# Starting the down projection one burst later in batch 2 of a fused attention and ReGLU kernel

## The chip, the cores and the metric

The kernel runs on one core of one Trainium2 chip. The metric is device time in microseconds of one launch. All inputs and the output are float32 in the chip's DRAM; the matrix products inside run on float16 tiles with float32 sums.

## The reference: what is computed

```python
# q, k, v: (8 batches, 12 heads, 448 positions, 64)
scores = scale * np.matmul(q, k.transpose(0, 1, 3, 2)) - np.log(S)      # scale = 1/8, S = 448
attn = 1.0 / (1.0 + np.exp(-scores))                                    # a sigmoid, no softmax
attn_out = np.matmul(attn, v)
x = attn_out.transpose(0, 2, 1, 3).reshape(B * S, H * D)                # (3584, 768)

# w_gate, w_val: (768, 1536), w_out: (1536, 768)
gate = np.maximum(x @ w_gate, 0.0)
val = x @ w_val
out = gate * val @ w_out                                                # (3584, 768)
```

For each batch there are scores, a sigmoid and a product with V (the attention), and then a feed-forward part: gate and value projections, their product h, and a down projection with `w_out`.

## The kernel before: the parts that matter

The order of instructions on TensorE is written by hand, batch after batch. Attention of batch b is interleaved with feed-forward work that earlier batches have left in two queues. A `gv` piece ("f" in the code) makes one 128-wide slice of h for one batch; there are 12 of them for each batch. A `down` tile ("y") makes 128 finished rows of the output from all 12 slices of h of a pair of batches; there are 7 of them for each pair, and the first pair is batches 0 and 1.

```python
def gv(b, q0, qn, f, act_relu):                      # "f"
    ps = []
    for nm, wt in (("g_ps", wg), ("v_ps", wv)):
        ps.append(bank(nm))
        for dc in range(NDC):                        # 6 matmuls each
            nc.tensor.matmul(ps[-1][:, 0:qn], wt[:, dc, f*P:(f+1)*P],
                             xT_tiles[(b, dc)][:, q0:q0+qn], start=..., stop=...)
    ...                                              # Relu on ScalarE, then VectorE writes hT
    nc.vector.tensor_tensor(out=hT_tiles[(g, f)][:, o:o+qn], in0=gate_sb[:, 0:qn],
                            in1=ps[1][:, 0:qn], op=AOP.mult)

def down(g, t):                                      # "y"
    ...
    for nm, m0, m1 in (("ya", 0, 512), ("yb", 512, DM)):
        ps = bank(nm)
        for f in range(NFC):                         # 12 matmuls each
            nc.tensor.matmul(ps[:, 0:m1-m0], hT_tiles[(g, f)][:, t*P:(t+1)*P],
                             wo[:, f, m0:m1], start=..., stop=...)
        nc.vector.tensor_scalar(out=ysb[:, m0:m1], in0=ps[:, 0:m1-m0], scalar1=OUT_SCALE, ...)
    store(g, t, ysb, 0, DM, (nc.sync, nc.sync))
```

`bank` hands out the eight PSUM banks in turn, two rings of four each. The weights `wo` of the down projection come in two transfers, columns 0 to 511 for `ya` and columns 512 to 767 for `yb`. They are issued by GpSimd late in batch 1, behind a small copy (`hold`) that waits for a transposed tile of batch 2, and behind V of batch 2:

```python
def load_o():
    for m0, m1 in ((0, 512), (512, DM)):
        nc.gpsimd.dma_start(wo[:, :, m0:m1], moe_w_out[:, m0:m1].rearrange("(c p) m -> p c m", p=P))

def hold(b, g):
    nc.gpsimd.tensor_copy(gate[0:1, :], qkT_tiles[(b, g)][0:1, 0, 0:2])

def late_loads():                                    # a hook in the last burst of batch 1
    dma_transposes(2, 1)
    hold(2, 1)
    load_v(2)
    load_o()
```

A batch is cut into six bursts, m = 0 to 5. A burst is three or four score units (`qk_unit`: 4 matmuls, then two sigmoids on ScalarE, for one chunk of 64 keys), with a product with V (`pv_group`) placed after the second unit in some bursts, and then the feed-forward pieces that `mix[m]` names:

```python
for b in range(1, B):
    cuts = (0, 3, 6, 9, 13, 17, 21) if b == 1 else (0, 4, 7, 11, 14, 18, 21)
    pv_at = {3: 0, 5: 1} if b == 1 else {0: -1, 2: 0, 4: 1}
    ...
    elif b == 2:
        mix = ["ff", "ff", "ffy", "ff", "ffy", "ffy"]
    elif b % 2:
        mix = ["ffy", "ffy", "ff", "ffy", "ff", "ffy"]
    else:
        mix = ["ffy", "ff", "ffy", "ff", "ffy", "ff"]
    for m in range(len(mix)):
        for i, (g, c) in enumerate(order[cuts[m] : cuts[m + 1]]):
            if i == 2 and m in pv_at:
                if m == 0: pv_finish(b - 1)
                else:      pv_group(b, pv_at[m])
            qk_unit(b, g, c)
        if m >= 4 and 1 < b < B - 1:
            dma_transposes(b + 1, m - 4)             # VectorE copies k, q to rel; SyncE issues the transpose
        if m == 0 and b > 1:
            dma_transposes(b, 2)
        ...
        elif m == 0 and b + 1 < B:
            if b == 2: hold(2, 2)
            load(b + 1, 0, 3, "kq")                  # k and q of the next batch, by GpSimd
            load_v(b + 1)
        ffn_mix(mix[m], hooks.get(m, ()))
```

After batch 7 whatever is left in the two queues is worked off.

Of the kernel before, what the change touches and what calls it, by code (L numbers as in the profile page):

```python
# [17 lines left out]
def kernel(  # L18
# [74 lines left out]
    def load(b, g0, g1, which, c0=0, c1=NCH):  # L93
        for nm, t16, src in zip("kq", tiles_of(b), (k, q)):
            if nm in which:
                xs, cs = slice(2 * g0, 2 * g1), slice(c0 * D, c1 * D)
                nc.gpsimd.dma_start(t16[:, xs, cs], rows_of(src, b)[:, xs, cs])  # L97

    def load_v(b):
        v16 = tiles_of(b)[2]  # L100
        nc.gpsimd.dma_start(v16[:, 0::2, :], rows_of(v, b)[:, 0::2, :])  # L101
        for r in range(2):
            nc.gpsimd.dma_start(  # L103
                v16[64 - 64 * r : P - 64 * r, 1::2, :], rows_of(v, b)[64 * r : 64 * r + 64, 1::2, :]
            )
# [95 lines left out]
    def dma_transposes(b, g):  # L201
        k16, q16, _ = in_tiles[b]
        rel = relp.tile([P, TW, P], FP16, tag="rel", name="rel")
        for ti, t16 in enumerate((k16, q16)):
            nc.vector.tensor_copy(
                rel[:, ti * NCH : (ti + 1) * NCH, :].rearrange("p c (h d) -> p h c d", h=2),
                t16[:, 2 * g : 2 * g + 2, :].rearrange("p h (c d) -> p h c d", c=NCH),
            )
        nc.sync.dma_start_transpose(
            qkT_of(b, g)[:], rel[:].rearrange("p c x -> p (c x)")  # L210
        )
# [68 lines left out]
    def qk_unit(b, g, c):  # L280
        ps = [bank("qk_ps") for _ in range(2)]
        qk(qkT_tiles[(b, g)], c, 0, NCH, lambda hh: ps[hh][:, 0:S])
        PT = PTp.tile([P, 2, 512], FP16, tag="PT", name="PT")
        for hh in range(2):
            sigmoid(PT[:, hh, 0:S], ps[hh][:, 0:S])
        PT_tiles[(b, g, c)] = PT

    def pv_group(b, g):
        pv(b, g, 0, S, [PT_tiles.pop((b, g, c))[:, :, 0:S] for c in range(NCH)])
# [81 lines left out]
    def ffn_mix(kinds, hooks=()):  # L371
        hooks = list(hooks)
        for left in range(len(kinds), -1, -1):
            while hooks and hooks[0][0] >= left:
                hooks.pop(0)[1]()
            if left:
                (gv_queue if kinds[len(kinds) - left] == "f" else y_queue).popleft()()
# [58 lines left out]
    def pv_finish(b):  # L436
        pv_group(b, NG - 1)
        push_gv(b, 0, S, range(NFC))
        if b % 2:
            push_down(b // 2, range(7))  # L440
# [5 lines left out]
    def hold(b, g):  # L446
        nc.gpsimd.tensor_copy(gate[0:1, :], qkT_tiles[(b, g)][0:1, 0, 0:2])

    def both(b, g):
        pe_transposes(b, g, 0)  # L450
        pe_transposes(b, g, 1)
# [8 lines left out]
# [3 lines that stand above are left out]
        hooks = {}  # L463
        if b == 1:
            mix = ["f" * n for n in (3, 3, 3, 3, 3, 2)]
            hooks = {
                1: [(1, lambda: both(1, 1))],
                3: [(1, lambda: both(1, 2))],
                4: [(3, lambda: dma_transposes(2, 0))],
                5: [(2, late_loads)],  # L470
            }
        elif b == 2:
            mix = ["ff", "ff", "ffy", "ff", "ffy", "ffy"]
        elif b % 2:
            mix = ["ffy", "ffy", "ff", "ffy", "ff", "ffy"]
        else:
# [4 lines that stand above are left out]
                    if m == 0:  # L481
                        pv_finish(b - 1)
                    else:
                        pv_group(b, pv_at[m])
                qk_unit(b, g, c)
            if m >= 4 and 1 < b < B - 1:
                dma_transposes(b + 1, m - 4)
            if m == 0 and b > 1:
                dma_transposes(b, 2)
            if b == 1:  # L490
                if m == 0:
                    load(2, 0, 1, "kq")
                    load(2, 1, 2, "kq")
                    load(2, 2, 3, "kq")
            elif m == 0 and b + 1 < B:
                if b == 2:
                    hold(2, 2)
                load(b + 1, 0, 3, "kq")
                load_v(b + 1)
            ffn_mix(mix[m], hooks.get(m, ()))  # L500
# [34 lines left out]
```

## Time and profile before

| what | value |
|---|---|
| time, median of 3 runs | 431.05 us (430.83 to 431.26) |
| span of the profiled execution | 429.5 us |
| TensorE matmuls (PE) | 418.5 us busy, 97% of the span |
| VectorE (DVE) | 141.8 us, 33% |
| ScalarE (ACT) | 201.1 us, 47% |
| GpSimd (POOL) | 49.8 us, 12% |
| granted TensorE clock | 1.000 |

In the profile's lines PE is the matmul stream of TensorE and PEld its weight loads, which overlap the matmuls. A name such as `ya<-wo,hT` means that the instructions write the tile `ya` and read `wo` and `hT`; L335 is the source line of the matmul in `down`, L297 that in `gv`, L222 that in the score units, L240 that in the product with V. "x12" counts instructions. A bracket at the end of a timeline line is the idle time of the engine ahead of that line, and what ended it. In a timeline the second column is how long the merged group lasted up to the modelled end of its last instruction, so that groups can overlap slightly.

### The profile page before, as it was taken

To read this page: it belongs to the slowest core of one execution; us is meant where nothing else is said; L and a number is where in the kernel's file an instruction comes from. 1 tells how busy PE (TensorE), PEld (TensorE's weight loads), DVE (VectorE), ACT (ScalarE), POOL (GpSimd) and SP (SyncE) were. 2 spreads that over 40 slices of the span, in tenths; PEclk is the share of its full clock that TensorE was granted. 3 is DMA by queue.
4 is the path that set the end of the run, shared out by engine and by line. 5 is a ranking of instruction groups with operands and counts; after the bars stand their busy time and mean duration, and the time that the engine had idled before them with its cause. 6 is when DMAs were issued, how large, how long until landed. Compare 5 with 4: busy or idle time off the path is not lost.

```text
span 429.5 us, 8576 instructions
## 1 busy us (share of the span) xinstructions
PE 418.5 (97%) x3668; PEld 231.9 (54%) x3668; DVE 141.8 (33%) x277; ACT 201.1 (47%) x424; POOL 49.8 (12%) x73
## 2 busy tenths in 40 slices
PE   8899999889999999999999999999999999999996
PEld 3677774345555455545545455545545554555563
DVE  2453443224233243233242243332442322322231
ACT  5766787434444454446443743473473446122000
POOL 9543204400030001200030000100000000000000
PEclk9999999999999999999999999999999999999999
DMA  9999958999799033951389114721243101100134
GB/s 147 198 202 203 203 81 131 203 220 195 110 155 182 0 81 82 169 104 38 85 122 182 46 43 82 127 56 38 44 88 75 37 2 38 37 2 0 46 102 110
DMA packets 68789, 43.63 MB, mean 102 GB/s; under 512 B 35600, under 2 KB 65168, under 8 KB 68752
## 3 DMA queue, kind: packets, MB, share of 16 engines
q0 software_dynamic: 30736, 23.37, 36.5%
q1 hardware_dynamic: 37664, 19.47, 22.7%
q8 instruction: 28, 0.46, 0.4%
q10 hardware_dynamic: 352, 0.26, 0.2%
q14 instruction: 9, 0.07, 0.1%
HBM read 47.19 MB, written 11.01 MB: 136 GB/s over the span
## 4 chain that ended last, share of the span: by engine, by line
PE 78%; DMA 13%; issue 5%; POOL 3%; DVE 0%; ACT 0%; POOLq 0%
PE g_ps L297 21%; PE v_ps L297 21%; PE ya L335 16%; PE yb L335 9%; PE qk_ps L222 6%; PE pv_ps L240 5%; DMA wo<-in_moe_w_out_dram 4%; DMA v<-in_v_dram 4%; DMA q<-in_q_dram 3%; DMA wg<-in_moe_w_gate_dram 2%; POOL k L97 1%; POOL q L97 1%; POOL v L103 1%; POOL v L101 0%; DVE xT L168 0%
## 5 line engine op out<-in xcount | busy, mean ns | idle before, releaser
L177 ACT ACTIVATE PT<-qk_ps 128x448 f16<-128x448 f32 (+3 forms) x318 | 151.6, 584 | 123.2 <-PE qk_ps L222 122.3
L297 PE MATMUL g_ps<-xT,wg 128*128 128x448 f16 (+2 forms) x648 | 127.5, 333 | 0.2 <-DVE xT L168 0.2
L297 PE MATMUL v_ps<-xT,wv 128*128 128x448 f16 (+2 forms) x648 | 126.8, 332 | 0.3 <-DMA wv<-in_moe_w_val_dram 0.3
L315 DVE TENSOR_TENSOR hT<-gate_sb,v_ps 128x448 f16<-128x448 f32 (+2 forms) x108 | 61.0, 569 | 164.5 <-PE v_ps L297 98.0
L335 PEld LDWEIGHTS <-hT 128*128 128x128 f16 x672 | 65.6, 98 | 50.6 <-DMA wo<-in_moe_w_out_dram 4.0
L297 PEld LDWEIGHTS <-wg 128*128 128x128 f16 x648 | 58.4, 98 | 56.5 <-issue 15.8
L297 PEld LDWEIGHTS <-wv 128*128 128x128 f16 x648 | 62.3, 98 | 47.9 <-DMA wv<-in_moe_w_val_dram 0.6
L306 ACT ACTIVATE gate_sb<-g_ps 128x448 f32<-128x448 f32 (+2 forms) x102 | 54.4, 544 | 70.8 <-PE g_ps L297 70.6
L335 PE MATMUL ya<-wo,hT 128*128 128x512 f16 x336 | 77.1, 379 | 1.9 <-DMA wo<-in_moe_w_out_dram 1.9
L222 PE MATMUL qk_ps<-qkT 64*64 64x448 f16 (+2 forms) x756 | 48.0, 336 | 1.9 <-ACT PT L177 1.1
L335 PE MATMUL yb<-wo,hT 128*128 128x256 f16 x336 | 41.3, 273 | 1.2 <-DMA wo<-in_moe_w_out_dram 1.2
L168 DVE TENSOR_SCALAR xT<-pv_ps 128x448 f16<-128x448 f32 (+2 forms) x54 | 28.4, 568 | 30.8 <-PE pv_ps L240 30.8
L343 DVE TENSOR_SCALAR ysb<-ya 128x512 f32<-128x512 f32 x28 | 19.4, 692 | 56.9 <-PE ya L335 55.0
L240 PE MATMUL pv_ps<-PT,v 64*64 64x448 f16 (+2 forms) x756 | 36.7, 329 | 0.0
L222 PEld LDWEIGHTS <-qkT 64*64 64x64 f16 x756 | 17.8, 105 | 21.6 <-issue 14.3
L240 PEld LDWEIGHTS <-v 64*64 64x64 f16 x756 | 21.6, 107 | 10.8 <-issue 0.5
L101 POOL DMA_DIRECT2D v<-in_v_dram x8 | 6.0, 747 | 174.2 <-PE qk_ps L222 173.9
L343 DVE TENSOR_SCALAR ysb<-yb 128x256 f32<-128x256 f32 x27 | 11.5, 425 | 18.1 <-PE yb L335 18.1
L349 ACT ACTIVATE ysb<-yb 128x256 f32<-128x256 f32 x1 | 0.4, 384 | 27.9 <-PE yb L335 27.9
L97 POOL DMA_DIRECT2D q<-in_q_dram x15 | 11.4, 760 | 8.8 <-PE trt L191 2.9
L97 POOL DMA_DIRECT2D k<-in_k_dram x14 | 10.9, 778 | 7.6 <-DMA wv<-in_moe_w_val_dram 3.5
L103 POOL DMA_DIRECT2D v<-in_v_dram x16 | 10.1, 635 | 2.6 <-DMA wg<-in_moe_w_gate_dram 2.3
(25 smaller groups left out, 59.4 us busy)
## 6 DMA issues: line engine op xcount, KB each, us to landing
out_dram<-ysb SPq DMA_DIRECT2D x54, 192.0 KB, 2.7
k<-in_k_dram POOLq DMA_DIRECT2D x5, 672.0 KB, 13.7
q<-in_q_dram POOLq DMA_DIRECT2D x5, 672.0 KB, 17.0
v<-in_v_dram POOLq DMA_DIRECT2D x8, 336.0 KB, 5.3
v<-in_v_dram POOLq DMA_DIRECT2D x16, 168.0 KB, 6.6
k<-in_k_dram POOLq DMA_DIRECT2D x8, 224.0 KB, 10.4
wo<-in_moe_w_out_dram POOLq DMA_DIRECT2D x1, 1536.0 KB, 15.4
q<-in_q_dram POOLq DMA_DIRECT2D x6, 224.0 KB, 11.2
```

The lines of the kernel that those rows point to most:

```text
L97: nc.gpsimd.dma_start(t16[:, xs, cs], rows_of(src, b)[:, xs, cs])
L101: nc.gpsimd.dma_start(v16[:, 0::2, :], rows_of(v, b)[:, 0::2, :])
L103: nc.gpsimd.dma_start(v16[64 - 64 * r : P - 64 * r, 1::2, :], rows_of(v, b)[64 * r : 64 * r + 64, 1::2, :])
L168: nc.vector.tensor_scalar(out=xT_of(b, pr)[:, q0 : q0 + qn], in0=src, scalar1=XSCALE, scalar2=None, op0=AOP.mult,)
L177: nc.scalar.activation(PT_ap, ps_ap, AF.Sigmoid, bias=sig_bias, scale=qk_scale)
L222: nc.tensor.matmul(out_of(hh)[o : o + 64, :], qkT[rows, c, cols], qkT[rows, NCH + c0 : NCH + c1, cols], start=True, stop=True, tile_positi ...
L240: nc.tensor.matmul(ps[hh][64 * r : 64 * r + 64, 0:qn], v16[rows, 2 * g + hh, c * D : (c + 1) * D], pieces[c][rows, hh, :], start=(c == 0), ...
L297: nc.tensor.matmul(ps[-1][:, 0:qn], wt[:, dc, f * P : (f + 1) * P], xT_tiles[(b, dc)][:, q0 : q0 + qn], start=(dc == 0), stop=(dc == NDC - 1),
L306: nc.scalar.activation(gate_sb[:, 0:qn], ps[0][:, 0:qn], AF.Relu)
L315: nc.vector.tensor_tensor(out=hT_tiles[(g, f)][:, o : o + qn], in0=gate_sb[:, 0:qn], in1=ps[1][:, 0:qn], op=AOP.mult,)
L335: nc.tensor.matmul(ps[:, 0 : m1 - m0], hT_tiles[(g, f)][:, t * P : (t + 1) * P], wo[:, f, m0:m1], start=(f == 0), stop=(f == NFC - 1),)
L343: nc.vector.tensor_scalar(out=ysb[:, m0:m1], in0=ps[:, 0 : m1 - m0], scalar1=OUT_SCALE, scalar2=None, op0=AOP.mult)
```

## The change

In batch 2 the mix of feed-forward work is reordered: the first down tile stands in burst 3 instead of burst 2, and the other two stay where they were, in bursts 4 and 5. It gives the two transfers of `wo` one burst more before the first matmul that reads them. Nothing is added or taken away.

```diff
         elif b == 2:
-            mix = ["ff", "ff", "ffy", "ff", "ffy", "ffy"]
+            mix = ["ff", "ff", "ff", "ffy", "ffy", "ffy"]
         elif b % 2:
```

The engines' instruction lists differ in only that: on TensorE the 24 matmuls of the first down tile, with their weight loads, come 36 matmuls later (12 of three score units and 24 of two `gv` pieces), and on VectorE the two copies of the tile out of PSUM come behind the two `hT` products of burst 3 instead of ahead of them. The lists of ScalarE, GpSimd and SyncE are the same in both kernels.

## The prediction

> **What bounds the kernel now.** I read the busy shares of the page first, then the list of what TensorE waited for, then TensorE's timeline around the longest of those waits, then the transfers and VectorE near it. The shares:
>
> ```profile
> PE 418.5 (97%) x3668; PEld 231.9 (54%) x3668; DVE 141.8 (33%) x277; ACT 201.1 (47%) x424; POOL 49.8 (12%) x73
> ```
>
> The matmul stream sets the time. The kernel can only gain by shorter matmuls or fewer gaps between them; this change leaves every matmul as it is, so only gaps count. The list of TensorE's waits over the whole kernel, in full but for its head:
>
> ```profile
> PE ya L335 <- DMA wo<-in_moe_w_out_dram: 1.9, 1, 1.9
> PE yb L335 <- DMA wo<-in_moe_w_out_dram: 1.2, 1, 1.2
> PE warm_ps L160 <- DVE zeros L116: 1.2, 1, 1.2
> PE qk_ps L222 <- ACT PT L177: 1.1, 4, 0.4
> PE qk_ps L222 <- DVE qkT L196: 0.8, 2, 0.5
> PE v_ps L297 <- DMA wv<-in_moe_w_val_dram: 0.3, 1, 0.3
> PE g_ps L297 <- DVE xT L168: 0.2, 1, 0.2
> PE trt L191 <- DVE k L383: 0.2, 1, 0.2
> ```
>
> The two largest are the first down tile waiting for the two halves of its weights, 3.1 us together. Asked by stretches, the same list puts all the others but one in the first 30 us (the `xT` one, 0.2 us, comes after 250 us). So after the start the kernel has one real hole. TensorE's timeline across it, then across burst 4, where a down tile does not wait (start, duration, engine, line, operation):
>
> ```profile
> 82.04 1.30 PE L297 MATMUL v_ps<-xT,wv 128*128 128x448 f16 x6
> 85.25 2.76 PE L335 MATMUL ya<-wo,hT 128*128 128x512 f16 x12 [1.91 <-DMA wo<-in_moe_w_out_dram]
> 89.22 1.48 PE L335 MATMUL yb<-wo,hT 128*128 128x256 f16 x12 [1.20 <-DMA wo<-in_moe_w_out_dram]
> 90.63 0.76 PE L222 MATMUL qk_ps<-qkT 64*64 64x448 f16 x12
> ...
> 95.97 0.57 PE L222 MATMUL qk_ps<-qkT 64*64 64x448 f16 x8
> ...
> 101.59 1.30 PE L297 MATMUL v_ps<-xT,wv 128*128 128x448 f16 x6
> 102.73 2.75 PE L335 MATMUL ya<-wo,hT 128*128 128x512 f16 x12
> 105.32 1.47 PE L335 MATMUL yb<-wo,hT 128*128 128x256 f16 x12
> 106.72 0.76 PE L222 MATMUL qk_ps<-qkT 64*64 64x448 f16 x12
> ```
>
> The reader should compare starts, not ends. In burst 4 `ya` begins 102.73 - 101.59 = 1.14 us after the last `v_ps` group, `yb` 2.59 us after `ya`, and the next scores 1.40 us after `yb`. In the waiting tile the same distances are 85.25 - 82.04 = 3.21, 89.22 - 85.25 = 3.97 and 1.41. The hole is thus (3.21 - 1.14) + (3.97 - 2.59) = 2.07 + 1.38 = 3.45 us, a little more than the 3.1 us of the wait list, which counts from modelled ends.
>
> **What the Trainium skill says.** "Perfetto Trace Analysis", section "Tensor Engine Instruction (MATMUL, LD_WEIGHTS)", says that a matmul's reported end is computed and not observed; the trace agrees, since 82.04 + 1.30 = 83.34 while an unhindered successor starts at 83.18. I therefore take the 3.45. "TensorE: Matmul & The Clock Gate", section "Back-to-back issue gap", gives N/2.4 + 2.5 ns for an isolated warm matmul, 215.8 ns at N = 512; here 2.59 us / 12 = 216 ns, so the tile itself has nothing left to lose. "PSUM — Partial Sum Buffer", section "Engine vs sequencer instructions", says that matmuls start in program order: so nothing behind the waiting tile could slip ahead, and the order has to be changed by hand. The trace agrees: no score matmul starts between 82.04 and 90.63. "DMA: Bandwidth & Descriptors", section "Anatomy of one DMA — SWDGE (gpsimd) path", says that waits happen on the issuing sequencer and that DMA engines only consume their queues; a load already issued is then not moved by a shift on TensorE. That fixes the landing times used below.
>
> **The change, part by part.** It removes and adds no instruction.
>
> First, the slot left empty. Burst 2's last `v_ps` starts at 82.04, and burst 3's scores follow it as scores follow a burst without a down tile: in burst 1 to 2 of the same batch, 76.42 - 75.19 = 1.23 us. They start at 82.04 + 1.23 = 83.27 instead of 90.63.
>
> Second, what now precedes the tile. Burst 3 takes 95.97 - 90.63 = 5.34 us from its scores to the next scores; 0.09 of it is the step from `gv` to scores (1.23 - 1.14), so `ya` can begin after 5.25 us, at 88.52, and `yb` at 88.52 + 2.59 = 91.11.
>
> Third, whether the weights are there. GpSimd issues the halves at 69.84 and 70.90; they take 15.4 and 18.3 us from issue to landing and land at 85.2 and 89.2 (the matmuls start within 0.1 us of that). Nothing ahead of 83.2 us differs between the kernels, so these times hold. Slack is 88.52 - 85.2 = 3.3 us for `ya` and 91.11 - 89.2 = 1.9 us for `yb`. Both waits vanish whole.
>
> Fourth, the sum. The tile takes 2.59 + 1.40 = 3.99 us, so burst 4's scores begin at 88.52 + 3.99 = 92.51 instead of 95.97: 3.46 us earlier, the hole again but for rounding. From there both orders are identical, and each later gap would have to be new to give something back. All of the gain lies on the path that sets the end, because TensorE runs without a hole from there to the last down tile.
>
> **The rivals.** The first: a load with a fixed arrival becomes the next wait. The candidates are k and q of batch 3, issued while `wo` is still moving; q is the later. Its issue on GpSimd, its time to landing (last column of the transfers issued in that stretch), and the copies on VectorE that read both:
>
> ```profile
> 79.63 0.83 POOL L97 DMA_DIRECT2D q<-in_q_dram x1
> ```
> ```profile
> q<-in_q_dram POOLq DMA_DIRECT2D x1, 672.0 KB, 17.0
> ```
> ```profile
> 98.97 0.38 DVE L205 COPY rel<-k 128x896 f16<-128x896 f16 x1
> 99.27 0.39 DVE L205 COPY rel<-q 128x896 f16<-128x896 f16 x1
> 100.73 0.62 DVE L315 TENSOR_TENSOR hT<-gate_sb,v_ps 128x448 f16<-128x448 f32 x1 [1.07 <-PE v_ps L297]
> ```
>
> q lands at 79.63 + 17.0 = 96.6. Today its copy comes 2.6 us later; after the shift it would want to start at 99.27 - 3.45 = 95.8 and so waits 0.8 us. This new wait I do expect. But it is VectorE's: it ends near 97.0, and the next product is due at 100.73 - 3.45 = 97.3. Even if q came 1 us later, the `hT` product only frees a PSUM bank eight groups on, over 4 us later. The transposed tile made from these copies, 9.5 us from issue to landing (so at about 107), is first read in batch 3's scores, at 115.96 - 3.45 = 112.5. I put the cost at 0; were it wrong and fully exposed, it would be 0.8 us, giving 428.4.
>
> The second: the hole gave ScalarE time to rest (8.3 us idle), and score units now come close behind `gv` pieces, so TensorE could wait for sigmoids to free PSUM banks; the list shows 1.1 us of that in four waits. Against it: those are in the first 30 us, and the step from burst 1 of batch 2 to burst 2, again three score units after `ff` with no tile between, shows no idle bracket, though ScalarE has eight sigmoids there (3.60 us in its timeline, 0.45 us each). If it came all the same, a wait like the largest there (0.4 us) would leave 428.0.
>
> The third: the `wo` landing is delayed, so that the tile waits again. For: the loads share the 16 DMA engines, and two of 192 KB each for the output are issued at 91.19, later in the new kernel. Against: stores come after `yb`, when `wo` is in. To lose all 3.45 us the second half would have to come 5.4 us late; I give that one chance in a hundred.
>
> The fourth: the tile only moves to where it hurts the tail. The queues are drained in the same order after batch 2, and the last tiles are the same, so the end is not touched.
>
> **Range and chances.** 431.05 - 3.45 = 427.6 us, which is 0.8% less. The three runs of before span 0.43 us, so noise of the median is some 0.2 us on each side; new small waits can only take from the gain, up to 0.8 us. I take 427.2 to 428.4. A gain over 2% would need 8.6 us, more than all of TensorE's waits together; a loss of 2% has no source. Chances: 0.01, 0.98, 0.01.
>
> **What would show it right or wrong.** In the changed kernel's waits of TensorE the two `wo` lines should be gone and nothing over 0.4 us should be new. The timeline should show burst 3's scores at about 83.3, `ya` at 88.5, `yb` at 91.1, burst 4's scores at 92.5, and a span near 426.0 instead of 429.5. On VectorE a wait of about 0.8 us for q ahead of its copy to `rel`, near 96.6, with no wait of TensorE behind it. The prediction is wrong if a line for `wo` stays, if scores start to wait for `PT`, or if burst 4 is 3.5 us early and the last tile is not.

## The result and the profile after

The changed kernel takes 427.89 us (median of 4 runs, 427.89 to 428.94) against 430.97 us (4 runs, 430.83 to 431.26) for the kernel before: 3.1 us less, a ratio of 0.9934 with a 95% interval of 0.9917 to 0.9951. The span of the profiled execution goes from 429.5 to 426.0 us.

The list of what TensorE waited for, in full, answers the list of the kernel before:

```profile
PE warm_ps L160 <- DVE zeros L116: 1.2, 1, 1.2
PE qk_ps L222 <- ACT PT L177: 1.1, 4, 0.4
PE qk_ps L222 <- DVE qkT L196: 0.8, 2, 0.5
PE g_ps L297 <- DVE xT L168: 0.2, 1, 0.2
PE v_ps L297 <- DMA wv<-in_moe_w_val_dram: 0.2, 1, 0.2
```

The two lines for `wo` are gone and no line is new. TensorE's timeline over the same place shows what filled the hole:

```profile
82.07 1.30 PE L297 MATMUL v_ps<-xT,wv 128*128 128x448 f16 x6
83.30 0.76 PE L222 MATMUL qk_ps<-qkT 64*64 64x448 f16 x12
...
87.41 1.30 PE L297 MATMUL v_ps<-xT,wv 128*128 128x448 f16 x6
88.54 2.75 PE L335 MATMUL ya<-wo,hT 128*128 128x512 f16 x12
91.13 1.47 PE L335 MATMUL yb<-wo,hT 128*128 128x256 f16 x12
92.53 0.57 PE L222 MATMUL qk_ps<-qkT 64*64 64x448 f16 x8
```

Burst 3's scores follow burst 2's `f` pieces at once, `ya` comes 1.13 us after the last `v_ps`, `yb` 2.59 us after `ya`, and no line has a bracket of idle time. Burst 4's scores start at 92.53 instead of 95.97, 3.44 us earlier. Nothing was given back over the remaining 325 us: the last down tile's `ya` starts 3.43 us earlier too. Before, then after:

```profile
421.44 2.75 PE L335 MATMUL ya<-wo,hT 128*128 128x512 f16 x12
```
```profile
418.01 2.75 PE L335 MATMUL ya<-wo,hT 128*128 128x512 f16 x12
```

On VectorE, the copies that read k and q of batch 3:

```profile
95.54 0.38 DVE L205 COPY rel<-k 128x896 f16<-128x896 f16 x1
96.08 0.39 DVE L205 COPY rel<-q 128x896 f16<-128x896 f16 x1 [0.16 <-DMA q<-in_q_dram]
97.29 0.62 DVE L315 TENSOR_TENSOR hT<-gate_sb,v_ps 128x448 f16<-128x448 f32 x1 [0.81 <-PE v_ps L297]
```

The wait for q is new, as foreseen, and is over 1.2 us before the next product.

### The profile page after: what moved, and what is told of

The parts are those of the page before. It is cut to its first block, busy times and chain, and to the rows that moved or that the text cites. A ratio compares the mean times of both kernels' runs of the same rounds, so it can differ in the third digit from the quotient of the medians.

```text
span 426.0 us, 8576 instructions
## 1 busy us (share of the span) xinstructions
PE 418.5 (98%) x3668; PEld 232.1 (54%) x3668; DVE 141.8 (33%) x277; ACT 200.9 (47%) x424; POOL 49.7 (12%) x73
## 4 chain that ended last, share of the span: by engine, by line
PE 93%; DMA 3%; POOL 2%; ACT 0%; DVE 0%; issue 0%; POOLq 0%; ACTq 0%
PE g_ps L297 26%; PE v_ps L297 25%; PE ya L335 17%; PE yb L335 9%; PE qk_ps L222 8%; PE pv_ps L240 7%; DMA wv<-in_moe_w_val_dram 3%; POOL q L97 1%; PE trt L191 1%; POOL k L97 1%; POOL wg L133 0%; POOL v L103 0%; DVE xT L168 0%; ACT PT L177 0%; POOL wv L134 0%
## 5 line engine op out<-in xcount | busy, mean ns | idle before, releaser
L343 DVE TENSOR_SCALAR ysb<-yb 128x256 f32<-128x256 f32 x27 | 11.5, 425 | 16.7 <-PE yb L335 16.7
## 6 DMA issues: line engine op xcount, KB each, us to landing
q<-in_q_dram POOLq DMA_DIRECT2D x5, 672.0 KB, 16.5
```

What stands on the lines that cost most here:

```text
L343: nc.vector.tensor_scalar(out=ysb[:, m0:m1], in0=ps[:, 0 : m1 - m0], scalar1=OUT_SCALE, scalar2=None, op0=AOP.mult)
```

## The experiments

The theory: the gain is the vanished wait for the two halves of `wo`, nothing else; what counts is when each half lands against when its matmuls come up. The main rival: the order of bursts is worth something by itself (a tile in burst 3 fits better, or more delay helps). A second rival: a late transfer elsewhere eats into the gain. All comparisons are with the kernel before, or with the changed kernel, run on the same chip in the same series where there was one; between series the kernel before stood at 430.97, 431.55, 431.28 and 431.28 us.

### The tile at two places inside burst 3

```diff
-            mix = ["ff", "ff", "ff", "ffy", "ffy", "ffy"]
+            mix = ["ff", "ff", "ff", "yff", "ffy", "ffy"]     # e3
+            mix = ["ff", "ff", "ff", "fyf", "ffy", "ffy"]     # e4
```

> The down tile placed in burst 3 right behind the three score units, ahead of both f pieces (yff). ya could begin at 83.3 + 0.7 = 84.0 us and waits 1.3 us for the first half (landing 85.3); yb could begin 2.59 later at 87.8 and waits until 89.2. Against the changed kernel the tile's end is 89.2 + 1.4 - (84.0 + 3.99) = 2.6 us late. Theory (only landing times count): 427.9 + 2.6 = 430.5 us, span 428.6. Rival (one burst of delay is what counts, the tile being in burst 3 either way): 427.9.

> The down tile in burst 3 between the two f pieces (fyf). ya begins at 84.0 + 2.27 = 86.3 us, after the first half is in: no wait. yb could begin at 88.85 and waits until 89.2 to 89.3. Theory: one wait for wo, of yb, 0.3 to 0.5 us, and 427.9 + 0.4 = 428.3 us, span 426.4. Rival: 427.9 with no wait, or 431 if the tile needs the whole burst ahead of it.

With the tile right behind the scores: 430.55 us (20 runs; ratio 0.9977, 0.9970 to 0.9985), span 428.4. Its timeline:

```profile
83.37 0.76 PE L222 MATMUL qk_ps<-qkT 64*64 64x448 f16 x12
85.09 2.76 PE L335 MATMUL ya<-wo,hT 128*128 128x512 f16 x12 [0.96 <-DMA wo<-in_moe_w_out_dram]
89.03 1.48 PE L335 MATMUL yb<-wo,hT 128*128 128x256 f16 x12 [1.17 <-DMA wo<-in_moe_w_out_dram]
90.35 1.30 PE L297 MATMUL g_ps<-xT,wg 128*128 128x448 f16 x6
```

By starts, `ya` waits 85.09 - 83.37 - 0.70 = 1.02 us (0.70 is the step from such scores to what follows them) and `yb` 89.03 - 85.09 - 2.59 = 1.35, together 2.37. The span is 428.4 - 426.0 = 2.4 us over the changed kernel's, and the median is 431.55 - 430.55 = 1.0 us under the kernel before. The tile stands in burst 3 here too and most of the gain is lost, so the burst is not what counts.

With the tile between the two `f` pieces: 428.66 us (4 runs, 428.06 to 429.25; ratio 0.9936, 0.9919 to 0.9954). In its profile `ya` starts at 87.44 and `yb` at 90.23, 2.79 us apart instead of 2.59, so 0.2 us of wait for the second half; the list of waits doesn't show it, since the modelled end of `ya` covers it. Expected were 0.3 to 0.5. The tile stands later than foreseen because this whole execution runs 1.2 us late; the issue of `wo`, at 71.04 instead of 69.89, is late with it. The median cannot carry a wait of 0.2 us, because its runs fall into two groups, 428.06 and 428.14 against 429.18 and 429.25. The profile is of the 429.25, and its list has waits at the start that the first profile of the changed kernel has not or has shorter: 0.6 us for `wv`, 0.4 for V, 0.2 for k.

### `wo` early, in both orders

```diff
     def late_loads():
         dma_transposes(2, 1)
         hold(2, 1)
         load_v(2)
-        load_o()
...
             if b == 1:
                 if m == 0:
                     ...
                     load(2, 2, 3, "kq")
+                    load_o()
```

> The old order of down tiles, but both wo transfers issued in burst 0 of batch 1, right behind k and q of batch 2, instead of behind V of batch 2. Estimated landing: k and q of batch 2 are in at 56.5 us, wo's 2304 KB at some 204 KB per us take 11.3 more, so about 68 us, before the first ya at 83.2. Theory (the gain is the vanished wait for wo and nothing else): no wait for wo, ya at 83.2, and 427.5 to 428.0 us, as in the changed kernel. Rival (the order of bursts itself is worth something): about 431. A side cost may come: the transposed tiles of batch 2 move while wo does, and batch 2's first scores at 64.2 us could wait 0 to 2 us for theirs, which would stand as a wait of the scores for a qkT transfer in the list.

> The new order of down tiles together with the early wo transfers. Theory: with wo in early there is nothing left for the order to gain, so this is within 0.3 us of the run with the old order and early wo, whatever side cost the early transfers have. Rival (the order is worth 3 us by itself): 3 us below that run.

Old order: 436.37 us (4 runs, 435.32 to 436.87; ratio 1.0112, 1.0094 to 1.0130). New order: 435.97 us (4 runs, 435.15 to 437.06; 1.0109, 1.0085 to 1.0133). The two are 0.40 us apart, a little more than the 0.3 expected, but their runs overlap: with `wo` in early, the order of the tiles makes no difference that can be measured, against 3.1 us without. That speaks for the theory. But the side cost was far above the 0 to 2 us that I had put. The first line of TensorE's waits in the run with the old order, and two stretches of its busy times inside that hole (after the busy time of each engine stand the granted clock, the DMA share and GB/s):

```profile
PE qk_ps L222 <- DMA qkT<-rel: 6.3, 1, 6.3
```
```profile
67.00:68.00 1.00, 0.00 (x0) 0.00 (x0) 0.00 (x0) 0.00 (x0) 0.00 (x0) 0.92 1.33 182
68.00:69.00 1.00, 0.00 (x0) 0.00 (x0) 0.00 (x0) 0.00 (x0) 0.00 (x0) 0.50 1.35 184
```

The transposed tile of batch 2's first scores took 14.6 us from issue to landing instead of 5.0 in the kernel before, while `wo` filled the DMA engines; the scores came at 71.04 instead of 64.7, where they would have followed in that execution. The `hold` in the kernel before keeps `wo` behind such a tile. And in that hole the granted clock fell to 0.50, so that the stretch from these scores to the next `f` piece then took 75.02 - 71.04 = 3.98 us instead of 66.44 - 64.23 = 2.21. The sum closes: 6.34 us of wait by starts and 1.77 of slow work, less the 3.45 us hole that is gone, make 4.66 us; the medians are 436.37 - 431.55 = 4.82 apart.

### The old order, with less ahead of `wo`

A gentler way to the same end: V of batch 2 stands ahead of `wo` in the queue, so it alone is moved early.

```diff
         hold(2, 1)
-        load_v(2)
         load_o()
...
                     load(2, 2, 3, "kq")
+                    load_v(2)
```

> The old order of down tiles; V of batch 2, which stands ahead of wo in the queue, is issued in burst 0 of batch 1 behind k and q instead. wo then starts some 2 to 3.4 us earlier: first half in at 82 to 83.4, second at 85.9 to 87.3 us. In the old order ya is due at 83.2 and yb at 85.8. Theory: ya waits 0 to 0.2 us, yb 0 to 1.5, and the time is 427.9 to 429.4 us, the gain of the change got without changing the order. Rival (order): 431. The transposed tile of batch 2's first scores may be held up behind V; it landed 14.6 us after issue behind 2304 KB of wo, and behind 672 KB I expect 8, which puts it at 64.0, just before the scores at 64.2.

428.38 us (4 runs, 428.02 to 428.60; ratio 0.9931, 0.9917 to 0.9946). The changed kernel, run again in the same series:

> The changed kernel unaltered, beside the next three on the same chip, as the mark they are read against. 427.9 us, 3.1 to 3.5 below the kernel before; some single runs 1.1 us longer, as one of the first four was (428.94).

428.34 us (4 runs, 427.84 to 429.14; ratio 0.9931, 0.9912 to 0.9950), which is 2.94 us below the kernel before and so under the 3.1 to 3.5 expected. The old order with an earlier `wo` is as fast as the new order. Its timeline:

```profile
81.94 1.30 PE L297 MATMUL v_ps<-xT,wv 128*128 128x448 f16 x6
83.07 2.75 PE L335 MATMUL ya<-wo,hT 128*128 128x512 f16 x12
85.94 1.48 PE L335 MATMUL yb<-wo,hT 128*128 128x256 f16 x12
87.36 0.76 PE L222 MATMUL qk_ps<-qkT 64*64 64x448 f16 x12
```

The tile is in burst 2, `ya` waits for nothing, and `yb` comes 2.87 - 2.59 = 0.28 us late: the second half, issued 1.03 us after 68.13, took 16.7 us and landed at 85.9. The transposed tile took 6.2 us here, so the scores at 64.13 did not wait. This, beside the pair above, rules the order out as a cause of its own, to within the scatter of a few tenths of a us.

### The two halves of `wo` swapped

```diff
-        for m0, m1 in ((0, 512), (512, DM)):
+        for m0, m1 in ((512, DM), (0, 512)):
             nc.gpsimd.dma_start(wo[:, :, m0:m1], ...)
```

> The new order of down tiles with the two wo transfers issued in the opposite order: columns 512 to 767 first, 0 to 511 behind them. Both are in at about 89.3 us. Theory (each half is a deadline of its own): ya, due at 88.5, now waits 0.7 to 0.8 us for its half, yb waits for nothing, and the time is 0.7 to 0.8 us over the changed kernel. Rival (3.3 us of slack on the first half is slack on the pair): no wait, no change.

In the new order: 428.77 us (428.46 to 429.14), which overlaps with the changed kernel's 427.84 to 429.14 beside it. This run settled nothing: in its profiled execution burst 3's scores began at 84.21, 0.9 us later than in the first profile of the changed kernel, while `wo` was issued only 0.45 us later (70.34), so that `ya` came up at 89.45 by itself and the half that landed at about 89.5 held it for 0.1 us at most. Hence the same swap in the old order, where the wait is too long to be masked:

> The old order of down tiles with columns 512 to 767 of wo loaded first and 0 to 511 behind them. In the old order ya is due at 83.2 us, 5 us and more before the landing, so the jitter of the start can't hide the wait. Theory (each half is a deadline of the matmuls that read it): ya waits until both halves are in, 89.2 to 89.5 us, yb for nothing; the tile ends 89.3 + 3.99 = 93.3 instead of 90.6 us, and the time is 2.7 us over the kernel before, about 434. Rival (what counts is when the pair is in, 89.2 either way): the time of the kernel before.

435.75 us (4 runs, 435.06 to 437.00; ratio 1.0109, 1.0087 to 1.0132), 4.5 us over the kernel before where 2.7 were expected. Its timeline, and the busy times by stretches around it (start and end, length, PE, PEld, DVE, ACT, POOL busy, then the clock, the DMA share and GB/s):

```profile
82.18 1.30 PE L297 MATMUL v_ps<-xT,wv 128*128 128x448 f16 x6
88.97 5.08 PE L335 MATMUL ya<-wo,hT 128*128 128x512 f16 x12 [5.49 <-DMA wo<-in_moe_w_out_dram]
93.89 1.47 PE L335 MATMUL yb<-wo,hT 128*128 128x256 f16 x12
95.29 0.76 PE L222 MATMUL qk_ps<-qkT 64*64 64x448 f16 x12
```
```profile
83.00:86.00 3.00, 0.47 (x3) 0.03 (x1) 0.62 (x1) 0.00 (x0) 0.37 (x1) 1.00 1.24 206
86.00:88.00 2.00, 0.00 (x0) 0.00 (x0) 0.00 (x0) 0.00 (x0) 0.00 (x0) 0.72 1.24 204
88.00:89.00 1.00, 0.03 (x1) 0.04 (x2) 0.00 (x0) 0.00 (x0) 0.00 (x0) 0.50 1.27 206
89.00:90.00 1.00, 1.00 (x3) 0.40 (x4) 0.00 (x0) 0.00 (x0) 0.00 (x0) 0.50 1.28 209
...
93.00:94.00 1.00, 1.00 (x5) 0.38 (x4) 0.00 (x0) 0.00 (x0) 0.00 (x0) 0.65 1.25 203
94.00:95.00 1.00, 1.00 (x12) 0.89 (x10) 0.69 (x1) 0.00 (x0) 0.00 (x0) 1.00 1.27 203
```

The wait is as the theory has it: `ya` starts when its half, now the second, lands, and `yb` waits for nothing. That `ya` then takes 93.89 - 88.97 = 4.92 us instead of 2.59 was not expected: the clock had fallen to 0.50 during the 5.5 us of idleness and did not come back before `ya` was nearly done. The account closes: burst 3's scores are 95.29 - 90.63 = 4.66 us later than in the kernel before. The slow `ya` is 2.33 of it, the longer hole 2.20 (88.97 - 82.18 - 1.14 = 5.65 by starts, instead of 3.45), and 0.14 stood ahead of the hole already (82.18 instead of 82.04).

### k and q of batch 3 later still

```diff
+                if b == 2:
+                    load_v(b + 1)
                 load(b + 1, 0, 3, "kq")
-                load_v(b + 1)
+                if b > 2:
+                    load_v(b + 1)
```

> The new order of down tiles with V of batch 3 loaded ahead of its k and q, so that q lands 672 KB, some 3.3 us, later, at about 99.3 instead of 96.0 us. VectorE's wait for q ahead of its copy grows from 0.2 to some 3.4 us, and the hT product due at 97.3 comes at 99.8. Theory (VectorE has slack here; its first bank is wanted again only after 103 us): no wait of TensorE for VectorE and the time of the changed kernel within 0.3 us; a wait of batch 3's first scores for their transposed tile of up to 0.8 us is possible, since that tile lands at 109.9 in the changed kernel and is due at 112.5. Rival (a late q shows in full): 2.5 us or more over the changed kernel.

428.28 us (427.92 to 429.77), beside 428.34 for the changed kernel in the same series. VectorE:

```profile
100.89 0.39 DVE L205 COPY rel<-q 128x896 f16<-128x896 f16 x1 [4.48 <-DMA q<-in_q_dram]
101.19 1.14 DVE L315 TENSOR_TENSOR hT<-gate_sb,v_ps 128x448 f16<-128x448 f32 x2
102.26 0.68 DVE L343 TENSOR_SCALAR ysb<-ya 128x512 f32<-128x512 f32 x1
```

VectorE waits 4.5 us for q, more than the 3.4 expected, since q came at about 100.9 and not at 99.3. Two products pile up behind it, and TensorE's list of waits has no entry for any of it: at 103.49 VectorE waits for TensorE again. The transposed tile, issued at 101.35, took 7.8 us and was in at 109.2, before batch 3's scores at 112.6. So the new wait that the change brings is harmless at 28 times its size.

### More delay, and both cures at once

```diff
-            mix = ["ff", "ff", "ff", "ffy", "ffy", "ffy"]
+            mix = ["ff", "ff", "ff", "ff", "ffyy", "ffy"]     # e10
```

> The first down tile moved on by one burst more, into burst 4 together with the second (ff, ff, ff, ff, ffyy, ffy). Theory (both halves were in before burst 3's tile, so more delay buys nothing): no wait for wo and the time of the changed kernel within 0.3 us, 428.0 to 428.5. Rival (later is better still): below 427.6.

> The new order of down tiles and V of batch 2 issued early, the two cures at once. Theory: they remove the same wait, so the gains do not add: the time of the changed kernel within 0.3 us (428.0 to 428.5), at best 0.2 to 0.3 us below the old order with V early, whose yb still came 0.3 us late. Rival (separate gains): 425.

One burst more of delay: 428.32 us (427.99 to 428.48). The new order together with V of batch 2 early: 428.02 us (427.94 to 428.11). The ratios to the kernel before, 0.9932 and 0.9927, are that of the changed kernel (0.9931) within their intervals of 0.0015 to 0.0019 on each side. Neither further delay nor the second cure adds what can be measured, and no version here beats the changed kernel clear of its scatter.

## Why the prediction was right

The bound: the matmul stream with one hole. Right; TensorE stays the bound (98% of the span), and the gain is a gap closed.

The size of the hole by starts, 3.45 us, rather than the 3.1 us of the wait list. Right for the execution it was read from: between the two profiles the spans differ by 3.5 us and the last tile moved by 3.43. As the size of the usual hole it was somewhat too large. The medians differ by 3.08 us in the first series and by 2.94 in the repeat. The profiled execution of before took 431.32 us, 0.35 more than that kernel's median, and that of after was exactly at its median; 431.32 - 427.89 = 3.43. I had taken 3.45 from a median that the profile was not of, which is why 427.6 came out 0.3 us low, inside the range of 427.2 to 428.4; the repeat's 428.34 is barely inside it. Other profiles suggest that the hole itself varies. Where a matmul waits for the second transfer, an estimate of the old order's hole is that start less the start of burst 2's last `v_ps`, less 1.14 + 2.59: 89.03 - 82.14 - 3.73 = 3.16 with the tile behind the scores, 90.23 - 83.24 - 3.73 = 3.26 with it between the `f` pieces, 88.97 - 82.18 - 3.73 = 3.06 in the old order with the halves swapped. The kernel before was profiled only once, so its usual hole was not measured.

The slack of the halves, 3.3 and 1.9 us. Right in the changed kernel, and the tile at three places shows the same sums at work: 2.4 us of wait right behind the scores (2.6 expected), 0.2 behind one `f` piece (0.4), none behind two.

The first rival, q of batch 3: the wait came, at 0.2 us instead of 0.8. q was issued at 79.53 and took 16.5 us, so it was in at 96.0 and not at 96.6. The transposed tile behind it was mis-sized the other way: it took 13.4 us from its issue near 96.5, not 9.5, and landed at about 109.9 instead of 107, which still left 2.6 us before batch 3's scores at 112.52. That the late q costs nothing is shown by the run with 4.5 us of it.

The second rival, sigmoids: no wait of scores for `PT` is new; the list has the same 1.1 us in four as before. ScalarE's longest idle stretch there shrank from 8.3 us to 4.8. One reading was wrong without harm: burst 2 of batch 2 has four score units with a product with V among them (hence the eight sigmoids), not three. The copy with three units behind `ff` is burst 1 (`qk_ps` x12 at 71.08), which has no idle bracket either.

The third rival, a late `wo`: it did not occur, but its pricing was incomplete. I said that all of the gain would be lost if the second half came 5.4 us late, a wait worth its own length. The swapped halves show that one long hole can be worth more: 5.5 us of idleness brought 2.3 us of slow matmuls after it. A wait of 3.45 us would be no shorter than the idleness after which the clock fell (2.7 to 3.4 us, see the last section), so less delay might have been enough; no run tried that. In the kernel before, with waits of 1.9 and 1.2 us and `ya` between them, the clock read 1.00 throughout.

The fourth rival, the tail: untouched, as said.

## What to carry to other kernels

When an in-order matmul stream waits for a load, take the size of the hole from starts against an unhindered copy of the same step, in more than one execution if the size matters to tenths of a us. Then ask only for which instructions could fill it and whether the load is in by the time that they are done; the gain ends there, and placing the consumer later, or loading earlier as well, adds nothing. Loading earlier is not free when the DMA engines are full: moving 2304 KB forward cost a wait of 6.3 us elsewhere, moving 672 KB cost nothing that could be measured. Issue the parts of a split load in the order in which they are read: in the reverse order waits of 1.9 and 1.2 us became one of 5.5, and 2.3 us of slow matmuls came on top. Whether two waits are cheaper than one of the same sum was not tried.

## What was not expected of the hardware

The clock drop. In the run with swapped halves TensorE's last matmul ahead of the hole ended at 83.48 (a modelled end); the mean of 0.72 from 86 to 88 us puts the fall to 0.50 at about 86.9, some 3.4 us into the hole, and the 0.65 from 93 to 94 puts the return at about 93.7, 4.7 us after matmuls began again. In the old order with `wo` early the same reading (0.92 from 67 to 68, 0.66 from 74 to 75) puts the fall 3.1 us into the hole and the return 3.6 us after it; in the new order with `wo` early (0.56 from 67 to 68, 0.53 from 73 to 74) they are 2.7 and 3.3 us. In each of the three the half rate lasted 6.8 us, so a clock that fell early came back early. The Trainium skill describes this in "TensorE: Matmul & The Clock Gate", section "What's actually happening": half rate after at least one idle window of about 3.4 us, full rate after at least one busy window of that length. The 6.8 us are as long as two such windows, and the returns, after 3.3 to 4.7 us of work, agree with it; two of the falls, after 2.7 and 3.1 us of idleness, came sooner than one such window, so here the measurement decides. The waits of 1.9 and 1.2 us in the kernel before caused no fall.

The scatter of the start. Single runs of the changed kernel lie up to 1.3 us apart (427.84 to 429.14). Its second profile has burst 3's scores at 84.10 instead of 83.30, and the delay is there well before: by 23 us the two executions are 1.1 us apart (0.3 of it goes at 24 us, where the first profile waits for `wv` in its turn). 0.26 us of it is there at 5.7 us, where a few transposes took longer; the rest comes with waits for V (0.24 us) and for `wv` (0.40 us) before 20 us, which the first profile has not at these places. Whether these loads cause the whole of the scatter was not tried. Since the issue of `wo` moves with the start (70.69 in the second profile, 0.80 us later like the scores), such a delay alone leaves the slack of `wo` as it is. In the profile with swapped halves in the new order the scores of burst 3 had lost another 0.3 us in burst 2, behind the issue, and with it most of the 0.7 us that the swap should have cost was hidden.
